# K and V loaded group by group in 32 KB runs, with scores without mask, in a decode step of attention beside an MLP

## The chip, the cores and the metric

The kernel runs on one core of a Trainium2 chip. A core has five engines that run side by side and meet through semaphores: TensorE (PE), VectorE (DVE), ScalarE (ACT), GpSimd (POOL) and SyncE (SP), and 16 DMA engines that bring data from HBM into SBUF (128 partitions). Matmuls write into PSUM (128 partitions, 8 banks of 512 fp32). The metric is the device time of one execution in microseconds.

## The reference

One token (batch 1, length 1, D = 1024) goes through an attention over the last 4096 positions of a cache and an MLP, side by side; everything is bf16 in HBM.

```python
def _A_ref(x, k_cache, v_cache, wq, wo):        # Hq 32, Hkv 4, Dh 128, W = 4096, Sk = 65536
    q = (x @ wq).reshape(B, Sq, Hq, Dh).transpose(0, 2, 1, 3)
    k = repeat(k_cache[:, :, Sk - W:, :], 8, axis=1)
    v = repeat(v_cache[:, :, Sk - W:, :], 8, axis=1)
    p = softmax(einsum("bhqd,bhkd->bhqk", q, k) * Dh ** -0.5)
    o = einsum("bhqk,bhkd->bhqd", p, v)
    return o.transpose(0, 2, 1, 3).reshape(B, Sq, Hq * Dh) @ wo
def _B_ref(x, w1, b1, w2, b2):                  # F = 3584
    y = layernorm(x)
    return gelu(y @ w1 + b1) @ w2 + b2
xn = layernorm(x)
return x + _A_ref(xn, ...) + _B_ref(xn, ...)
```

The bytes that have to come in are wq 8 MB, K 4 MB, V 4 MB, w1 7 MB, W2 7 MB, wo 8 MB (MB of 1024 KB). Eight query heads share one of the four groups of K and V.

## The kernel before

All engines' programs are written out by hand, with semaphores between them. There is no scheduler: each engine runs its instructions in the order of the text, and the order of the transfers is the order in which SP issues them.

**The queue.** SP issues, in this order: wq's first half (`WQ_CHUNKS`, 4 MB), the first pair of groups of K (`load_k(0)`, L232), wq's second half, the second pair of K, w1 in one piece, then, after a wait for the last transpose of K (L311), the two pairs of V (L313, into the tile `KV` that K has left), after a wait for q the two chunks of W2 (16 and 12 of 28 rows per partition, into wq's place), and after a wait for h the five chunks of wo (L320; 8, 12, 9, 2 and 1 of 32 rows per partition). A row here is one of the 2 KB rows that a partition holds of W2 or wo. The three short rows x, b2 and b1 are issued by ACT; b1 comes as 128 pieces of 56 bytes.

**K and V before.** `pairs` lays a pair of groups over 128 partitions: partition 2m + g holds 64 positions of group g in one run of 16 KB. So a partition of a pair belongs to one of two groups, alternately.

```python
def pairs(cache, c):
    return cache[0, 2 * c:2 * c + 2, SK - W:SK, :].rearrange("g (m i) d -> m g (i d)", m=64)
```

**Start.** Two matmuls spread x over the partitions, DVE normalises it twice (L245 to L275), and writes the columns into `XZ` (for q) and `YZ` (for h). POOL makes constants. Matmuls with `HOT` (the `edge` function) clear PSUM banks 7, 0 and 1 before sums are added there.

**q and scores.** 64 matmuls give q in bank 7 (L449). DVE turns K in 32 by 32 blocks, in four pieces of 4096 columns (`turn_k`, L285): two for the first pair, then one, then the last behind q's turn. q is turned and spread into `QBD` (L305, L307). Four matmuls write a mask into banks 3 to 6 (`OTHER`, `ALT`, L455), 32 matmuls add the scores (L465) in 2048 columns. DVE takes the maximum (L334 to L343), ACT the exponential with its sums (L346), and DVE turns P into `PT` (L350), which lies at the end of `KT`.

**h.** 56 matmuls (L487) with w1, turned by four small matmuls (L494), with b1 added by DVE (L356) and the gelu behind it, give the first columns of `GO`.

**o and the output.** 32 matmuls of P and V (L502) in 8 turns of 4; DVE scales and picks (L383, L389); four small matmuls turn the result (L513) and ACT spreads it into `GO` and `OT`. W2 and wo are multiplied in rounds of 4 rows, 8 matmuls each, summed in bank 7: four rounds of W2, the turning of o, then three more of W2 and five of wo (`TURN`, `ROUNDS`; L523). POOL waits for the chunks and feeds PE's counter `s_feed`. The last 12 rows of wo (`TAIL` = 20) are multiplied by small matmuls of 32 columns, four side by side (L541), as their chunks land; the wo rows from 20 on lie in `KT`. Then ACT and DVE copy the sum out (L400) and SP stores it (L402).

Of the kernel before, what the change touches and what calls it, by code (L numbers as in the profile page):

```python
# [9 lines left out]
D = 1024  # L10
# [13 lines left out]
WO_CHUNKS = [8, 12, 9, 2, 1]  # L24
WO_HEAD = 2
XW = 136
PAIRS = 2
FAR = -1e30
XP = 72
TAIL = 20  # L30
# [5 lines left out]
ROUNDS = 12  # L36
TURN = 4
# [15 lines left out]
def bass_parallel_sum__sliding_block_cached__mixer_channel_mlp__decode_kernel(  # L53
# [19 lines left out]
    def sems(name, n):  # L73
        return [nc.alloc_semaphore(f"{name}{i}") for i in range(n)]

    s_x, s_b1, s_b2, s_v, s_out = (nc.alloc_semaphore(n) for n in ("s_x", "s_b1", "s_b2", "s_v", "s_out"))
    s_w1 = sems("s_w1", len(W1_CHUNKS))
    s_wq = sems("s_wq", len(WQ_CHUNKS))
    s_k = sems("s_k", PAIRS)
# [7 lines left out]
        "x", "h", "hT", "q", "sc", "pv", "tot", "o2", "fin")}  # L87
# [11 lines left out]
    B64 = sb("B64", [128, 64], f32)  # L99
    HALF4 = sb("HALF4", [64, 4], f32)  # L100
    HALF = sb("HALF", [64, PAIRS], f32)
    OTHER = sb("OTHER", [2, 128], bf16)
    ALT = sb("ALT", [2, 512], bf16)
    HOT = sb("HOT", [1, 8 + 128], bf16)
    EDGE = sb("EDGE", [2, 132], bf16)
    XBRP = sb("XBRP", [2, 16 * XP], bf16)
    B1T = sb("B1T", [128, FC], bf16)
# [8 lines left out]
    QBD = sb("QBD", [128, PAIRS * 512], bf16)  # L116
    HT = sb("HT", [128, FC], f32)
    U2 = sb("U2", [128, FC], f32)
    MX2 = sb("MX2", [128, 2], f32)
    MX8 = sb("MX8", [32, 8], f32)  # L120
    MXR = sb("MXR", [32, 1], f32)
    NMB = sb("NMB", [128, 1], f32)
# [6 lines left out]
    REC = sb("REC", [64, 1], f32)  # L129
    ON = sb("ON", [32, DH], bf16)  # L130
    GO = sb("GO", [128, ROUNDS * STEP + LEAD + 96], bf16)
    OT = GO[:, ROUNDS * STEP + LEAD:]
    ONM = QBD[0:32, :].bitcast(f32)
    KV = sb("KV", [128, 16384], bf16)
    KT = sb("KT", [128, 16384], bf16)
    PT = KT[:, 16384 - 2112:16384]
# [14 lines left out]
    def wo_home(row):  # L151
        return (BIG, (FC + row) * D) if row < TAIL else (KT, (row - TAIL) * D)
# [19 lines left out]
    act.dma_start(B1T[:, :], B_b1.rearrange("(p c) -> p c", c=FC)).then_inc(s_b1, 16)  # L172

    def pool_wait():
# [4 lines left out]
    POOL.mark(pool.memset(identb[:, :], 0.0))  # L179
    pool_wait()  # L180
# [5 lines left out]
    POOL.mark(pool.memset(HOT[:, :], 0.0))  # L186
    pool_wait()
    C["hot"] = POOL.mark(pool.memset(HOT[:, 7:8], 1.0))
# [3 lines left out]
    POOL.mark(pool.memset(QBD[:, :], 0.0))  # L192
    POOL.mark(pool.memset(HALF4[:, :], 1.0))
    POOL.mark(pool.memset(OTHER[:, :], FAR))
    POOL.mark(pool.memset(ALT[:, :], 0.0))
# [12 lines left out]
    POOL.mark(pool.affine_select(  # L208
        out=OTHER[:, :].rearrange("p (x g h) -> p x g h", g=2, h=REP),
        in_=OTHER[:, :].rearrange("p (x g h) -> p x g h", g=2, h=REP),  # L210
        pattern=[[0, 8], [-1, 2], [0, REP]], compare_op=ALU.not_equal, fill=0.0, base=0, channel_multiplier=1))
    POOL.mark(pool.affine_select(
        out=ALT[:, :].rearrange("p (x g) -> p x g", g=2), in_=ALT[:, :].rearrange("p (x g) -> p x g", g=2),
        pattern=[[0, 256], [-1, 2]], compare_op=ALU.not_equal, fill=1.0, base=0, channel_multiplier=1))
    POOL.mark(pool.affine_select(
        out=HALF4[:, :], in_=HALF4[:, :], pattern=[[-16, 4]], compare_op=ALU.is_ge, fill=0.0,
        base=0, channel_multiplier=1))
    pool_wait()
    POOL.mark(pool.affine_select(
        out=HALF4[:, :], in_=HALF4[:, :], pattern=[[16, 4]], compare_op=ALU.is_ge, fill=0.0,  # L220
        base=15, channel_multiplier=-1))
    POOL.mark(pool.memset(GO[:, :], 0.0))
    pool_wait()
    POOL.mark(pool.tensor_tensor(out=HALF[:, :], in0=HALF4[:, 0:2], in1=HALF4[:, 2:4], op=ALU.add))
    C["consts"] = POOL.cnt


    def pairs(cache, c):
        return cache[0, 2 * c:2 * c + 2, SK - W:SK, :].rearrange("g (m i) d -> m g (i d)", m=64)

    def load_k(c):
        sp.dma_start(KV[:, c * 8192:(c + 1) * 8192], pairs(A_k_cache, c)).then_inc(s_k[c], 16)  # L232

    load_chunks(WA, wq_p, WQ_CHUNKS[:1], NQ, s_wq)
    load_k(0)
    load_chunks(WA, wq_p, WQ_CHUNKS[1:], NQ, s_wq[1:], WQ_CHUNKS[0])
    load_k(1)
# [5 lines left out]
    def layernorm_stats(src, n, name):  # L243
# [15 lines left out]
    layernorm_stats(PS[:, 0:1024], 0, "ln1")  # L259
    DVE.mark(dve.tensor_scalar(out=XN[:, :], in0=PS[:, 0:1024], scalar1=MV[:, 0:1], scalar2=SD[:, 0:1],  # L260
# [18 lines left out]
        out=B64[:, :].rearrange("p (k r) -> p k r", k=2),  # L279
        in_=identf[:, :].rearrange("p (q r) -> p r q", q=4).unsqueeze(1).to_broadcast([128, 2, 32, 4]),  # L280
        axis=AX.X, op=ALU.add))

    def turn_k(n):
        dve.wait_ge(s_k[n // 2], 16)
        C["kt", n] = DVE.mark(dve.transpose(KT[:, n * 4096:(n + 1) * 4096], KV[:, n * 4096:(n + 1) * 4096]))  # L285

    for n in range(3):
        turn_k(n)
# [7 lines left out]
    dve.wait_ge(POOL.sem, C["consts"])  # L296
    act.wait_ge(POOL.sem, C["consts"])
    QD = QBD[:, :].rearrange("p (c e b h) -> p c e b h", c=PAIRS, e=4, b=4)
    QS = QTB.rearrange("p (j e c) -> p e c j", j=4, e=4)
    for b in range(4):  # L300
        for c in range(PAIRS):
            to = QD[32 * b:32 * b + 32, c, :, b, 16 * c:16 * c + 16].rearrange("p e (u j) -> p e u j", j=4)
            of = QS[32 * b:32 * b + 32, :, 4 * c:4 * c + 4, :]
            if PAIRS * b + c < 5:
                C["d_QBD"] = DVE.mark(dve.tensor_copy(to, of))  # L305
            else:
                C["a_QBD"] = ACT.mark(act.activation(out=to, in_=of, func=ACTF.Copy))  # L307
    turn_k(3)

    V = KV[:, :]  # L310
    sp.wait_ge(DVE.sem, C["kt", 3])  # L311
    for c in range(PAIRS):
        sp.dma_start(V[:, c * 8192:(c + 1) * 8192], pairs(A_v_cache, c)).then_inc(s_v, 16)  # L313
# [4 lines left out]
    for j, n in enumerate(WO_CHUNKS):  # L318
        home, first = wo_home(c0)
        sp.dma_start(home[:, first:first + n * D], wo_flat[:, c0 * D:(c0 + n) * D]).then_inc(s_wo[j], 16)  # L320
        c0 += n
# [9 lines left out]
    S = PS[:, 3 * 512:7 * 512]  # L331
    for n in range(2):
        dve.wait_ge(done["sc"], 14 + 2 * n)
        C["mx"] = DVE.mark(dve.tensor_reduce(  # L334
            out=MX2[:, n:n + 1], in_=S[:, 1024 * n:1024 * n + 1024], axis=AX.X, op=ALU.max))
    dve_wait()
    for b in range(4):
        DVE.mark(dve.tensor_copy(MX8[:, 2 * b:2 * b + 2], MX2[32 * b:32 * b + 32, :]))
    dve_wait()
    DVE.mark(dve.tensor_reduce(out=MXR[:, :], in_=MX8[:, :], axis=AX.X, op=ALU.max))  # L340
    dve_wait()
    for b in range(4):
        C["nmb"] = DVE.mark(dve.tensor_scalar(  # L343
            out=NMB[32 * b:32 * b + 32, :], in0=MXR[:, :], scalar1=-SCALE, scalar2=None, op0=ALU.mult))
    act.wait_ge(DVE.sem, C["nmb"])
    C["exp"] = ACT.mark(act.activation(  # L346
        out=Pb[:, :], in_=S, func=ACTF.Exp, bias=NMB[:, 0:1], scale=SCALE, accum_out=SUMP[:, 0:1]))

    dve.wait_ge(ACT.sem, C["exp"])
    C["d_pt"] = DVE.mark(dve.transpose(PT[:, 0:2048], Pb[:, :]))  # L350
# [4 lines left out]
    dve.wait_ge(s_b1, 16)  # L355
    DVE.mark(dve.tensor_tensor(  # L356
        out=HT[:, :].rearrange("p (t c) -> p c t", c=4),
        in0=PS[:, 2 * 512 + 32:2 * 512 + 64].rearrange("p (c t) -> p c t", c=4)[:, :, 0:7],
        in1=B1T[:, :].rearrange("p (t c) -> p c t", c=4), op=ALU.add))
# [18 lines left out]
    DVE.mark(dve.reciprocal(out=REC[:, :], in_=PS[0:64, 2 * 512 + 64:2 * 512 + 65]))  # L378
    dve_wait()
    dve.wait_ge(done["pv"], 8)  # L380
    for i in range(2):
        rows = slice(32 * i, 32 * i + 32)
        DVE.mark(dve.scalar_tensor_tensor(  # L383
            out=ONM.rearrange("p (i c d) -> p i c d", i=2, c=PAIRS)[:, i],
            in0=PS[rows, 512:1024].rearrange("p (c i d) -> p i c d", c=PAIRS, i=2)[:, i], scalar=REC[rows, 0:1],
            in1=HALF[rows, :].unsqueeze(2).to_broadcast([32, PAIRS, DH]), op0=ALU.mult, op1=ALU.mult))
    dve_wait()
    with nc.allow_low_precision(reason="one of the four terms is not zero"):
        C["on"] = DVE.mark(dve.tensor_reduce(  # L389
            out=ON[:, :], in_=ONM.rearrange("p (g d) -> p d g", g=4), axis=AX.X, op=ALU.add))  # L390
    act.wait_ge(done["o2"], 1)
    o2 = PS[:, 2 * 512:2 * 512 + 32]
    ACT.mark(act.activation(out=spread(FC // ROUND, TAIL // ROUND), in_=rows_of(o2[:, 0:TAIL]), func=ACTF.Copy))
    C["OT"] = ACT.mark(act.activation(
        out=OT[:, LEAD:LEAD + 2 * (32 - TAIL):2], in_=o2[:, TAIL:32], func=ACTF.Copy))
# [11 lines left out]
    pool.sem_inc(s_feed, 1)  # L407
    pool.wait_ge(s_wq[1], 16)
    pool.sem_inc(s_feed, 1)
    pool.wait_ge(DVE.sem, C["kt", 1])  # L410
    pool.sem_inc(s_feed, 1)
    pool.wait_ge(DVE.sem, C["kt", 3])
    pool.sem_inc(s_feed, 1)
    for semaphores, chunks in ((s_w2, W2_CHUNKS), (s_wo, WO_CHUNKS[:WO_HEAD])):
        if semaphores is s_wo:
            pool.wait_ge(ACT.sem, C["OT"])
        for semaphore, n in zip(semaphores, chunks):
            pool.wait_ge(semaphore, 16)
            pool.sem_inc(s_feed, n // ROUND)  # L419
    pool.wait_ge(s_wo[WO_HEAD], 16)  # L420
    pool.sem_inc(s_feed, 1)

    pe.wait_ge(POOL.sem, C["ones"])
    pe.wait_ge(s_x, 16)
    for i in range(2):
        last = pe.matmul(bank(i), lhsT=onesb[0:1, :], rhs=XB[0:1, 8 * i:8 * i + 8, :])  # L426
# [148 lines left out]
```

## Time and profile before

| what | value |
|---|---|
| median of 3 runs | 99.21 us (99.12 to 99.42) |
| profiled execution | 99.2 us, span 97.6 us |
| PE / DVE / POOL / ACT busy | 71.6 / 37.9 / 10.2 / 8.1 us |
| bytes read | 39.86 MB, 409 GB/s over the span |
| DMA share of the queue of SP | 95.7% of 16 engines' span |

The span runs from the first to the last instruction of the program in one profiled execution; the execution's own time is 1.6 us longer. Engines overlap, so busy times don't add up to the span. In the rows, `L433` is the line of the helper `add`, through which nearly all matmuls go; they are told apart by their tiles: `BIG,XZ` is q, `KT,QBD` scores, `BIG,YZ` h, `KV,KT` the product with V, `BIG,GO` the rounds of W2 and wo, `KT,GO` the last rows of wo. `SPq` is SP issuing a transfer, and `<-` names what an instruction waited for.

### The profile page before, as it was taken

What the parts mean: (1) busy time and instruction counts of PE and PEld (TensorE: products, weight loads), DVE (VectorE), ACT (ScalarE), POOL (GpSimd) and SP (SyncE); (2) the same over time, 40 slices, a digit from 0 to 9 for tenths busy, and PEclk for the clock granted to TensorE, in tenths of its full rate; (3) what the DMA queues carried; (4) which work ended last, traced back from release to release, by engine and by line L of the source; (5) the groups of instructions that cost most, each with busy time, mean ns of one, the idle gap of its engine ahead of it and who ended that gap; (6) DMA issues with size and microseconds to landing.
All of it is one profiled execution on the core that took longest, in us unless ns stands there. A gap on an engine that the chain in (4) does not pass through costs nothing.

```text
span 97.6 us, 1259 instructions
## 1 busy us (share of the span) xinstructions
PE 71.6 (73%) x337; PEld 30.1 (31%) x349; DVE 37.9 (39%) x50; ACT 8.1 (8%) x16; POOL 10.2 (10%) x29
## 2 busy tenths in 40 slices
PE   0005000399999973879979999799989999997991
PEld 0001000033444320323334444333344444443450
DVE  0001899899930699950581800050043000000001
ACT  0500000600000023000008000200000010000001
POOL 6999600000000000000000000000000000000000
PEclk9999999999999999999999999999999999999999
DMA  7599999999999998888999999999899998999980
GB/s 215 228 431 444 410 432 437 430 430 443 417 430 464 682 400 376 376 376 376 430 437 430 437 497 443 443 430 400 373 464 423 430 480 363 453 436 416 438 329 1
DMA packets 2229, 39.88 MB, mean 409 GB/s; under 512 B 434, under 2 KB 436, under 8 KB 692
## 3 DMA queue, kind: packets, MB, share of 16 engines
q1 hardware_dynamic: 2020, 39.85, 95.7%
q10 hardware_dynamic: 208, 0.01, 0.1%
q8 instruction: 1, 0.02, 0.1%
HBM read 39.86 MB, written 0.00 MB: 409 GB/s over the span
## 4 chain that ended last, share of the span: by engine, by line
DMA 79%; PE 13%; SPq 4%; issue 1%; DVE 0%
DMA BIG<-in_B_w_dram 47%; DMA KT<-in_A_wo_dram 32%; PE PS L433 13%; SPq L320 2%; SPq L232 1%; SPq L159 1%; DVE Pb L400 0%
## 5 line engine op out<-in xcount | busy, mean ns | idle before, releaser
L433 PE MATMUL PS<-BIG,GO 128*128 x84 | 20.1, 379 | 1.4 <-POOLq L419 0.5
L285 DVE STREAM_TRANSPOSE KT<-KV 128x4096 bf16<-128x4096 bf16 x4 | 17.6, 4432 | 4.8 <-DMA KV<-in_A_k_cache_dram 4.8
L433 PE MATMUL PS<-BIG,XZ 128*128 x64 | 16.2, 418 | 0.0
L433 PEld LDWEIGHTS PS<-BIG,GO 128*128 x96 | 9.3, 98 | 11.8 <-issue 1.7
L433 PE MATMUL PS<-BIG,YZ 128*128 x56 | 12.4, 380 | 0.7 <-DMA BIG<-in_B_w_dram 0.7
L433 PE MATMUL PS<-KT,QBD 128*128 x32 | 8.0, 379 | 2.6 <-DVE QBD L305 1.8
L433 PEld LDWEIGHTS PS<-BIG,XZ 128*128 x64 | 6.7, 105 | 9.9 <-issue 4.5
L400 DVE CAST Pb<-PS 64x256 bf16<-64x256 f32 x1 | 0.4, 417 | 21.7 <-PE PS L433 21.7
L433 PE MATMUL PS<-KV,KT 128*128 x32 | 8.3, 381 | 0.6
L430 PE MATMUL PS<-XBRP,HOT 1*128 1x512 bf16 x3 | 1.7, 620 | 9.0 <-DVE XZ L275 9.0
L433 PEld LDWEIGHTS PS<-BIG,YZ 128*128 x56 | 5.4, 96 | 7.5 <-issue 1.9
L426 PE MATMUL PS<-XBRP,onesb 1*128 1x512 bf16 x2 | 1.0, 605 | 8.2 <-DMA XBRP<-in_A_x_dram 8.2
L433 PEld LDWEIGHTS PS<-KT,QBD 128*128 x32 | 3.1, 96 | 7.5 <-issue 5.4
L245 DVE BATCH_NORM_STATS2 BN<-PS 128x6 f32<-128x512 f32 x2 | 1.3, 689 | 9.3 <-PE PS L426 9.3
L433 PEld LDWEIGHTS PS<-KV,KT 128*128 x32 | 3.1, 96 | 5.4 <-issue 3.9
L334 DVE TENSOR_REDUCE MX<-PS 128x1 f32<-128x1024 f32 x2 | 2.4, 1220 | 4.4 <-PE PS L433 4.4
L383 DVE SCALAR_TENSOR_TENSOR QBD<-PS,REC,HALF 32x256 f32<-32x256 f32 x2 | 0.9, 473 | 7.0 <-PE PS L433 6.9
L430 PEld LDWEIGHTS PS<-XBRP,HOT 1*128 1x128 bf16 x3 | 0.3, 118 | 10.2 <-DVE XZ L275 9.9
L350 DVE STREAM_TRANSPOSE KT<-Pb 128x2048 bf16<-128x2048 bf16 x1 | 2.3, 2312 | 2.1 <-ACT Pb L346 2.1
L356 DVE TENSOR_TENSOR HT<-PS,B1T 128x28 f32<-128x28 f32 x1 | 0.2, 209 | 7.4 <-PE PS L494 7.4
L346 ACT ACTIVATE Pb<-PS,NMB 128x2048 bf16<-128x2048 f32 x1 | 2.0, 1967 | 13.0 <-DVE NMB L343 13.0
L426 PEld LDWEIGHTS PS<-XBRP,onesb 1*128 1x128 bf16 x2 | 0.1, 98 | 8.2 <-issue 8.2
(76 smaller groups left out, 37.6 us busy)
## 6 DMA issues: line engine op xcount, KB each, us to landing
BIG<-in_A_wq_dram SPq DMA_DIRECT2D x2, 4096.0 KB, 18.9
BIG<-in_B_w_dram SPq DMA_DIRECT2D x1, 7168.0 KB, 46.0
KV<-in_A_k_cache_dram SPq DMA_DIRECT2D x2, 2048.0 KB, 23.2
KV<-in_A_v_cache_dram SPq DMA_DIRECT2D x2, 2048.0 KB, 13.4
BIG<-in_B_w_dram SPq DMA_DIRECT2D x1, 4096.0 KB, 24.6
BIG<-in_B_w_dram SPq DMA_DIRECT2D x1, 3072.0 KB, 31.2
BIG<-in_A_wo_dram SPq DMA_DIRECT2D x1, 3072.0 KB, 25.6
KT<-in_A_wo_dram SPq DMA_DIRECT2D x1, 2304.0 KB, 30.6
```

What stands on the lines that cost most here:

```text
L159: sp.dma_start(dst[:, c0 * width:(c0 + n) * width].rearrange("p (c n) -> p c n", c=n), src[:, c0:c0 + n, :],).then_inc(semaphores[j], 16)
L232: sp.dma_start(KV[:, c * 8192:(c + 1) * 8192], pairs(A_k_cache, c)).then_inc(s_k[c], 16)
L245: DVE.mark(dve.bn_stats(out=BN[:, 12 * n + 6 * i:12 * n + 6 * i + 6], in_=src[:, 512 * i:512 * i + 512]))
L285: C["kt", n] = DVE.mark(dve.transpose(KT[:, n * 4096:(n + 1) * 4096], KV[:, n * 4096:(n + 1) * 4096]))
L320: sp.dma_start(home[:, first:first + n * D], wo_flat[:, c0 * D:(c0 + n) * D]).then_inc(s_wo[j], 16)
L334: C["mx"] = DVE.mark(dve.tensor_reduce(out=MX2[:, n:n + 1], in_=S[:, 1024 * n:1024 * n + 1024], axis=AX.X, op=ALU.max))
L346: C["exp"] = ACT.mark(act.activation(out=Pb[:, :], in_=S, func=ACTF.Exp, bias=NMB[:, 0:1], scale=SCALE, accum_out=SUMP[:, 0:1]))
L350: C["d_pt"] = DVE.mark(dve.transpose(PT[:, 0:2048], Pb[:, :]))
L383: DVE.mark(dve.scalar_tensor_tensor(out=ONM.rearrange("p (i c d) -> p i c d", i=2, c=PAIRS)[:, i], in0=PS[rows, 512:1024].rearrange("p (c ...
L426: last = pe.matmul(bank(i), lhsT=onesb[0:1, :], rhs=XB[0:1, 8 * i:8 * i + 8, :])
L430: pe.matmul(bank(n), lhsT=HOT[:, 8:136], rhs=XB[0:1, 0:8, :], start=True, stop=False, skip_group_check=True)
L433: return pe.matmul(to, lhsT=lhsT, rhs=rhs, start=False, stop=False, skip_group_check=True, **place)
```

## The change

- K and V are each loaded by four DMAs, one for each group, into 32 partitions: partition 32g + m holds 128 positions of group g in one run of 32 KB. All four loads of K stand between wq's two halves and share one semaphore, for which DVE waits once; the four transposes of K follow in a row.
- Scores take no mask. `QZ` holds q so that each block of 32 output partitions belongs to one group; there are 1024 columns of scores, in banks 4 and 5, still 32 matmuls. The maximum goes through two 32 by 32 transposes.
- P becomes block-diagonal: POOL clears 4096 columns of `PT` (now the start of `KT`) after the scores, and four transposes of 32 partitions by 1024 columns write the blocks. The product with V has 32 matmuls in 4 turns of 8.
- o is scaled, picked, reduced and turned by DVE alone (six steps), without matmuls.
- ACT clears the PSUM banks by three copies in place of matmuls with `HOT`.
- b1 comes in 32 pieces of 224 bytes and is turned and added by four matmuls with `E4` ahead of the h sums.
- wo comes in 16, 11, 4 and 1 rows, all into `BIG`; the rounds are 11 (seven of W2, four of wo) in one loop, and 16 rows are left to the small matmuls.

The order of the transfers becomes: wq's first half, K (4 loads), wq's second half, w1, V (4 loads), W2 (2), wo (4).

The diff, cut to its core:

```diff
-WO_CHUNKS = [8, 12, 9, 2, 1]
-WO_HEAD = 2
+WO_CHUNKS = [16, 11, 4, 1]
+WO_HEAD = 1
-TAIL = 20
+TAIL = 16
-ROUNDS = 12
-TURN = 4
+ROUNDS = 11
...
-    act.dma_start(B1T[:, :], B_b1.rearrange("(p c) -> p c", c=FC)).then_inc(s_b1, 16)
+    act.dma_start(B1R[:, :], B_b1.rearrange("(p c) -> p c", p=32)).then_inc(s_b1, 16)
...
+    act.wait_ge(POOL.sem, C["QZ"])
+    for first in (0, 4):
+        ACT.mark(act.activation(out=PS[:, first * 512:(first + 2) * 512].rearrange("p (b n) -> p b n", b=2),
+                                in_=QZ[:, 0:512].unsqueeze(1).to_broadcast([128, 2, 512]), func=ACTF.Copy))
+    ACT.mark(act.activation(out=bank(7), in_=QZ[:, 0:512], func=ACTF.Copy))
...
-    def load_k(c):
-        sp.dma_start(KV[:, c * 8192:(c + 1) * 8192], pairs(A_k_cache, c)).then_inc(s_k[c], 16)
+    def load_groups(cache, semaphore):
+        for g in range(HKV):
+            sp.dma_start(KV[32 * g:32 * g + 32, :], cache[0, g, SK - W:SK, :].rearrange(
+                "(m i) d -> m (i d)", m=32)).then_inc(semaphore, 16)
 
     load_chunks(WA, wq_p, WQ_CHUNKS[:1], NQ, s_wq)
-    load_k(0)
+    load_groups(A_k_cache, s_k)
     load_chunks(WA, wq_p, WQ_CHUNKS[1:], NQ, s_wq[1:], WQ_CHUNKS[0])
-    load_k(1)
     load_chunks(W1, w1_p, W1_CHUNKS, F, s_w1)
...
-    def turn_k(n):
-        dve.wait_ge(s_k[n // 2], 16)
-        C["kt", n] = DVE.mark(dve.transpose(KT[:, n * 4096:(n + 1) * 4096], KV[:, n * 4096:(n + 1) * 4096]))
+    dve.wait_ge(s_k, 64)
+    for n in range(4):
+        C["kt"] = DVE.mark(dve.transpose(KT[:, n * 4096:(n + 1) * 4096], KV[:, n * 4096:(n + 1) * 4096]))
...
-    sp.wait_ge(DVE.sem, C["kt", 3])
-    for c in range(PAIRS):
-        sp.dma_start(V[:, c * 8192:(c + 1) * 8192], pairs(A_v_cache, c)).then_inc(s_v, 16)
+    sp.wait_ge(DVE.sem, C["kt"])
+    load_groups(A_v_cache, s_v)
...
-    C["d_pt"] = DVE.mark(dve.transpose(PT[:, 0:2048], Pb[:, :]))
+    dve.wait_ge(POOL.sem, C["consts"] + 1)
+    for g in range(4):
+        C["d_pt"] = DVE.mark(dve.transpose(
+            PT[32 * g:32 * g + 32, :].rearrange("p (i y) -> p i y", y=128)[:, :, 32 * g:32 * g + 32],
+            Pb[32 * g:32 * g + 32, 0:1024].rearrange("p (i m) -> p i m", m=32)))
...
+    pool.wait_ge(done["sc"], 4)
+    POOL.mark(pool.memset(PT, 0.0))
```

## Prediction

> **What bounds the kernel now.** I read the page's head, slices and queues first, then the chain that ended last, the waits of the DMA queue, and the timeline around the end and around the clock's steps.
>
> ```profile
> span 97.6 us, 1259 instructions
> PE 71.6 (73%) x337; PEld 30.1 (31%) x349; DVE 37.9 (39%) x50; ACT 8.1 (8%) x16; POOL 10.2 (10%) x29
> GB/s 215 228 431 444 410 432 437 430 430 443 417 430 464 682 400 376 376 376 376 430 437 430 437 497 443 443 430 400 373 464 423 430 480 363 453 436 416 438 329 1
> q1 hardware_dynamic: 2020, 39.85, 95.7%
> HBM read 39.86 MB, written 0.00 MB: 409 GB/s over the span
> DMA 79%; PE 13%; SPq 4%; issue 1%; DVE 0%
> ```
>
> One queue, SP's, moves all 39.85 MB and is busy for 95.7% of the span; no compute engine comes near. The rate is flat from the third slice to the last but one.
>
> ```profile
> SPq L313 <- DVE KT L285: 39.0, 1, 39.0
> SPq L320 <- PE PS L433: 16.9, 1, 16.9
> ```
>
> SP issues each transfer long before its turn, so these waits cost nothing. V is issued at 42.94 us and w1, ahead of it, is still arriving at 49.0; wo is issued at 62.16 and W2 runs until 75.7.
>
> ```profile
> 49.68 12.45 PE L433 MATMUL PS<-BIG,YZ 128*128 x56 [0.68 <-DMA BIG<-in_B_w_dram]
> 88.56 5.13 PE L433 MATMUL PS<-BIG,GO 128*128 x21 [0.53 <-POOLq L419]
> 93.81 1.48 PE L433 MATMUL PS<-KT,GO 128*32 128x256 bf16 x44
> 95.52 0.29 PE L433 MATMUL PS<-KT,GO 128*32 128x256 bf16 x4 [0.22 <-DMA KT<-in_A_wo_dram]
> ```
>
> At the end PE is only just behind: each row waits for a wo chunk. So the time is the sum of the queue's packets plus about 2.4 us of end. The packet records of the trace give that sum. All 16 DMA engines work at once, and in each size nearly every packet takes the same time: 2 KB 84 ns, 4 KB 159, 16 KB 611, 18 KB 686, 24 KB 912, 32 KB 1213, 56 KB 2116. Every 128-row load gives each engine 8 packets. Per engine: wq, and W2's first chunk, 3 x 1213; K and V, 4 x 611; w1 2116; W2's second chunk 912; wo 611 + 912 + 686 + 159 + 84 = 2452: together 11,563, times 8 = 92.5 us. The first packet starts at 1.84, the first ones take up to 2173 ns, and the last lands at 95.18: the sum closes to 0.1 us. The span adds 2.37 us behind that, and the execution's 99.2 us is 1.6 over its span; it equals the median, 99.21.
>
> **The change, part by part.**
>
> *K and V loads.* Before, a K or V load writes all 128 partitions in 16 KB runs; after, it writes 32 partitions in 32 KB runs, four loads in a row. Each of the 16 engines gets 2 packets of 32 KB per load, 8 for K and 8 for V. If a packet keeps its 1213 ns, K and V cost 16 x 1213 = 19.4 us instead of 32 x 611 = 19.55: a gain of 0.14. But the trace has no large load into a quarter of the partitions. Its rows do not say whether 27.0 GB/s per engine is a limit of the stream or of the place it writes to, because in every big load each engine has 8 of the 128 partitions to itself. So the packet is bounded from both sides: 1213 ns if the limit is in the stream; 4 x 1213 = 4852 ns if it is in the place, and 16 streams crowd on a quarter of the places. A gain beyond 0.14 us is excluded, since no packet in the trace is faster than its size class. I take the mildest crowding that there can be, two streams on one place, 2426 ns, midway between the ends by ratio. I take crowding rather than none because times equal to the nanosecond over all 128 packets of a load, with 16 engines running, look like a fixed path that each stream owns, and the new loads take the separateness of the partitions away: all engines write group 0 together, then group 1, then 2, then 3. They keep step, because all have equal packets in the same order; the trace shows them at most 0.5 us apart where one load ends and the next begins. So loads queued behind cannot fill in. Added per engine: 16 x 1213 = 19.4 us.
>
> [...]
>
> *wo in 16, 11, 4, 1.* Per engine 1213 + 838 (686 x 22/18) + 310 (2 x 159, less a little) + 84 = 2445, against 2452: 8 x 7 ns = 0.06 us less.
>
> *The queue's sum.* 19.4 - 0.14 - 0.06 = +19.2 us; the last packet lands at 114.4 instead of 95.2.
>
> *Whether the queue ever runs dry.* K ends at 12.64 + 19.4 = 32.0. DVE now waits for all four K loads at once; behind that wait on DVE lie the four KT transposes and, behind them, the q transpose. Four at 4.43 us (L285) end at 50.1. SP's V issue waits for them, and w1 runs until 58.7, so 8 us are spare. Four K issues in place of one put about 2 us of SP work ahead of wq's second half, which is not due before 32. W2 waits behind V for q: wq's second half lands at 41.7, and 32 matmuls take 6.9 us at 215 ns, 13.7 at 427, so at most 56. wo waits for h: scores, then h's 12.45 us, end by 79, and W2 runs until 95. All covered. The cover for V is the thinnest: gone, each late microsecond costs one.
>
> *Scores, softmax, P.* The 32 score matmuls stay; 4 mask matmuls (1.03 us) and half the score columns go. Two maxima of 1.22 us become one, eight small copies and scalings (1.4) become two small transposes, a reduce and a scaling (about 0.8); the exponential over 1024 instead of 2048 columns takes 1.0 instead of 1.97. New: POOL clears 4096 columns of PT after the scores, 3.7 us by XZ's 0.99 for 1088, and behind it on POOL are only the feeds for W2, due at 87; four transposes of P of 1024 columns, 1.16 each by L350's 2312 for 2048, together 4.6 instead of 2.3. PV needs P only when V is there (78), so 15 us cover this. PV in 4 turns of 8 instead of 8 of 4 saves four loop gaps of 0.24 us; V's landing sets its start. The o chain is now six DVE steps and no matmuls, about 3 us, and its result is needed at 105.
>
> *Start.* Three ACT copies clear PSUM (1.0, 1.0 and 0.6 us by L346's rate) and the built code has one more table load (1.28). They start near 2.8 and end near 8; ACT's first square root is due at 10.85. The two edge matmuls ahead of q (1.03) go. POOL loses its 2.3 us select on ALT and some memsets. None of it touches the queue. b1 in 32 pieces makes 96 fewer packets of about 11 ns over 16 engines: under 0.1 us.
>
> *The end.* wo's first chunk now lands 9.8 us before the last packet, T. With the 0.74 us from landing to PE seen at 88.56, four rounds of 8 matmuls at 215 ns end at T - 2.2; the 11-row chunk (44 small matmuls, 1.45 us) at T - 0.75; the 4-row chunk, there at T - 0.15, at T + 0.4; the last row was there at T + 0.34 before. So +0.06 us.
>
> *PE's clock.* With DMA stretched, PE rests from 101.0 (24 matmuls after W2's last chunk) to 105.3. The rows:
>
> ```profile
> 20.00 0.15 PEld L433 LDWEIGHTS PS<-BIG,XZ 128*128 x1 [0.28 <-issue]
> 20.43 0.15 PEld L433 LDWEIGHTS PS<-BIG,XZ 128*128 x1 [0.28 <-issue]
> 39.30 0.91 PE L433 MATMUL PS<-KT,QBD 128*128 x3 [1.76 <-DVE QBD L305]
> ```
>
> After 9 us of rest matmuls run 427 ns apart until 23.84; after 1.76 us they run at 215. A rest of 4.3 us is nearer the second; I take no loss. If half speed returns, up to 4 to 5 us of the 6.9 us of rounds double, and with the slack of the end it costs up to 2.0 us, which I keep for the range. [...]
>
> **Sum.** 99.2 + 19.2 + 0.06 = 118.5 us.
>
> **Rivals.**
>
> *Streams keep their rate (not slower).* The limit is in the engine, so a packet takes 1213 ns wherever it goes. Then the queue's sum falls by 0.2, the end adds 0.06: 99.0 us. For it: 27.0 GB/s holds for all sizes and rows. Against: no row has several engines on one place. It decides if a 32 KB packet of K takes under 1250 ns. PE is then the second bound: q's second half could not start before 32.7 instead of about 28, scores end near 52, h near 64.8, PV near 73.4, W2's rounds near 85.4, while wo's first chunk is ready at 86.1; 0.7 us are spare, so with a slow clock after the rest of 6 us in q it could be 99.0 to 99.8.
>
> *A quarter.* Each engine's share of a 32-row load falls on the same few places: 4852 ns a packet, +58 us, 157 us. For it: 32 of 128 partitions is a quarter. Against: the two rows of an engine need not lie at the places of the others.
>
> *Something between or late.* A crowding that the engines partly evade, or V late: 103 to 117 or 121 to 140.
>
> **Chances.** Two on a place 0.68, full rate 0.20, quarter 0.06, between or late 0.06. What a measurement of this kernel can tell from no change is about 0.3%, 0.3 us. Full rate splits into 0.04 faster, 0.11 same, 0.05 slower; all else is slower: 0.04, 0.11, 0.85. The likeliest case's own range is 117.6 (the engines' 0.5 us of skew used once at each of K and V) to 121 (the clock falls, packets slightly over double). To leave out no more than 2 in 10 the range must reach to the full rate: 98.9 to 121.
>
> **What would show it.** Right: K's four loads landing about 19 us after wq's first half, near 32 us; slices of about 215 GB/s there and again for V between 59 and 78; slices over 400 elsewhere; V issued near 50; a chain that still ends in wo's last row. Wrong: K landed near 22 and rates over 400 throughout (full rate), or K landed near 51 (quarter); a queue idle between w1 and V would put the cost on DVE's transposes and not on the loads.

## The result and the profile after

The changed kernel takes 121.69 us (median of 6, 121.0 to 122.72) against 99.23: a ratio of 1.227, 95% interval 1.2208 to 1.2331. Slower, as forecast; the forecast of 118.5 is 3.2 us short, and the range, which goes to 121, ends 0.7 us too early. The profiled execution (122.72, the slowest of the six) has a span of 121.4.

The page's head, the granted clock and the rates in 40 slices of 3.03 us, the queue, and the chain that ended last:

```profile
span 121.4 us, 1227 instructions
PEclk9999999999755555996799999965799999965799
GB/s 173 411 455 379 314 173 173 216 227 248 173 410 453 459 491 302 605 302 605 173 173 227 238 227 173 173 345 443 421 432 397 456 443 421 443 393 438 391 165 1
q1 hardware_dynamic: 1684, 39.85, 94.9%
DMA 58%; PE 34%; issue 2%; SPq 2%; DVE 1%; ACT 1%; POOLq 0%
```

The same 39.85 MB, the same queue at 95%, but two valleys near 200 GB/s: slices 6 to 11, where K arrives, and 20 to 26, where V does. Between them the rate is what it was. SP's waits and the timeline around V's issue show that the queue did not run dry:

```profile
SPq L209 <- DVE KT L266: 46.9, 1, 46.9
```

```profile
33.63 17.42 DVE L266 STREAM_TRANSPOSE KT<-KV 128x4096 bf16<-128x4096 bf16 x4 [14.62 <-DMA KV<-in_A_k_cache_dram]
51.08 1.72 SPq L209 DMA_DIRECT2D KV<-in_A_v_cache_dram  x4
```

V is issued at 51.1 and w1, ahead of it, ends at 59.7. By the packet records, K's and V's packets of 32 KB take 2564 ns (median; wq's 1213 in the same trace), so the last packet lands at 116.85 instead of 95.18: +21.67. The end behind it takes 4.55 us instead of 2.37: +2.18. Together 23.85, the difference of the spans. The timeline of the end:

```profile
107.84 1.46 PE L403 MATMUL PS<-BIG,GO 128*128 x3 [4.20 <-POOLq L393]
108.24 0.15 PEld L403 LDWEIGHTS PS<-BIG,GO 128*128 x1 [0.15 <-issue]
108.67 0.15 PEld L403 LDWEIGHTS PS<-BIG,GO 128*128 x1 [0.27 <-issue]
109.09 0.15 PEld L403 LDWEIGHTS PS<-BIG,GO 128*128 x1 [0.28 <-issue]
117.75 1.65 PEld L403 LDWEIGHTS PS<-BIG,GO 128*32 128x32 bf16 x64 [0.42 <-issue]
119.73 0.42 DVE L376 CAST Pb<-PS 64x256 bf16<-64x256 f32 x1 [25.93 <-PE PS L403]
```

PE rests 4.2 us before wo's first round and then loads weights every 427 ns, the slow spacing of the start of the kernel before. The `PEclk` row has the same at its right end: 9, 6, 5, 7, 9. So wo's rounds end at 117.7, after the last packet, and all 64 small matmuls come behind it.

### The profile page after: what moved, and what is told of

It is laid out like the page before. It is cut to its first block, busy times and chain, and to the rows that moved or that the text cites. A ratio compares the mean times of both kernels' runs of the same rounds, so it can differ in the third digit from the quotient of the medians.

```text
span 121.4 us, 1227 instructions
## 1 busy us (share of the span) xinstructions
PE 76.0 (63%) x339; PEld 32.1 (26%) x350; DVE 40.9 (34%) x48; ACT 10.8 (9%) x19; POOL 9.3 (8%) x21
## 3 DMA queue, kind: packets, MB, share of 16 engines
q1 hardware_dynamic: 1684, 39.85, 94.9%
## 4 chain that ended last, share of the span: by engine, by line
DMA 58%; PE 34%; issue 2%; SPq 2%; DVE 1%; ACT 1%; POOLq 0%
PE PS L403 34%; DMA BIG<-in_A_wq_dram 33%; DMA BIG<-in_A_wo_dram 25%; SPq L209 2%; DVE Pb L271 1%; ACT Pb L269 0%; ACT QZ L282 0%; DVE Pb L376 0%; SPq L153 0%; POOLq L393 0%; POOLq L385 0%
## 5 line engine op out<-in xcount | busy, mean ns | idle before, releaser
L403 PE MATMUL PS<-BIG,XZ 128*128 x64 | 19.4, 478 | 25.0 <-POOLq L385 14.8
L403 PE MATMUL PS<-BIG,GO 128*128 (+1 forms) x141 | 23.8, 353 | 5.1 <-POOLq L393 4.2
L403 PEld LDWEIGHTS PS<-BIG,GO 128*128 (+1 forms) x152 | 10.9, 102 | 18.2 <-issue 11.7
L403 PE MATMUL PS<-KV,KT 128*128 x32 | 9.6, 476 | 3.4 <-DMA KV<-in_A_v_cache_dram 3.4
L403 PE MATMUL PS<-KT,QZ 128*128 x32 | 8.7, 438 | 1.2 <-ACT QZ L282 1.2
L387 POOL MEMSET KT<- 128x4096 bf16 x1 | 3.5, 3518 | 57.9 <-PE PS L403 57.9
L324 DVE STREAM_TRANSPOSE KT<-Pb 32x1024 bf16<-32x1024 bf16 x4 | 4.9, 1236 | 1.4 <-ACT Pb L318 1.3
L403 PEld LDWEIGHTS PS<-KT,QZ 128*128 x32 | 3.5, 110 | 6.3 <-issue 3.7
L306 DVE TENSOR_REDUCE MX<-PS 128x1 f32<-128x1024 f32 x1 | 1.2, 1225 | 9.4 <-PE PS L403 9.4
L318 ACT ACTIVATE Pb<-PS,NMT 128x1024 bf16<-128x1024 f32 x1 | 1.1, 1114 | 13.1 <-DVE NMT L316 13.1
## 6 DMA issues: line engine op xcount, KB each, us to landing
KV<-in_A_v_cache_dram SPq DMA_DIRECT2D x4, 1024.0 KB, 21.7
```

The source lines that it names most:

```text
L306: DVE.mark(dve.tensor_reduce(out=MX[:, 0:1], in_=S, axis=AX.X, op=ALU.max))
L318: C["exp"] = ACT.mark(act.activation(out=Pb[:, 0:1024], in_=S, func=ACTF.Exp, bias=NMT[:, 0:1], scale=SCALE, accum_out=SUMP[:, 0:1]))
L324: C["d_pt"] = DVE.mark(dve.transpose(PT[32 * g:32 * g + 32, :].rearrange("p (i y) -> p i y", y=128)[:, :, 32 * g:32 * g + 32], Pb[32 * g:3 ...
L387: POOL.mark(pool.memset(PT, 0.0))
L403: return pe.matmul(to, lhsT=lhsT, rhs=rhs, start=False, stop=False, skip_group_check=True, **place)
```

## The experiments

Theory (**place**): a load into 32 neighbouring partitions gives the 16 engines half as many places to write to, two engines share one, and packets take twice as long: an assumption made from 2564 ns against 1213. Rivals: **run** (the 32 KB run, or that all engines read one group's 1 MB), **number** (each further load costs), **rest** (the rest of the change), and for the end: the slow **clock** against the 16 rows of small matmuls.

**The loads alone.** `cut_rows` is the kernel before with each pair load cut in four:

```diff
-        sp.dma_start(KV[:, c * 8192:(c + 1) * 8192], pairs(A_k_cache, c)).then_inc(s_k[c], 16)
+        for b in range(4):
+            sp.dma_start(KV[32 * b:32 * b + 32, c * 8192:(c + 1) * 8192], pairs(A_k_cache, c)[16 * b:16 * b + 16]).then_inc(s_k[c], 16)
```

(V likewise; the waits count four loads. In the kernels below, too, the waits count the loads.)

> The kernel before with one thing changed: each of its four loads of K and V is cut by rows into four loads of 32 partitions; every byte still comes from and goes to the same place, in the same 16 KB runs. Place theory (32 partitions give 16 engines only half the places to write to): the 16 KB packets of K and V take 1282 ns instead of 611, half of the 2564 ns that 32 KB packets took in the changed kernel, so the queue grows by 32 x 0.67 = 21.5 us: 120.5 to 122.5, and 32 KB packets of wq stay at 1213. Run theory (what costs is a run of 32 KB, or one group's 1 MB read by all engines at once): 99.2 to 99.5, packets at 611. Number theory (each further load costs by itself): 12 further loads; if they cost what 16 loads cost in the changed kernel, 1 to 2 us each, 111 to 123, with packets unchanged at 611 and gaps between loads.

Measured: 120.61 us, ratio 1.2169 (1.2095 to 1.2244). 16 KB packets of K and V take 1262 to 1277 ns instead of 611, wq's stay at 1213. The slices of the page:

```profile
GB/s 176 353 519 364 260 194 231 375 353 518 298 226 198 325 463 309 559 366 309 408 220 209 209 231 198 226 369 353 518 369 455 422 408 430 446 455 409 409 270 1
```

The valleys are there with the same bytes, places and runs as in the kernel before. Run is out.

`cut_cols` makes as many loads, but over all partitions:

```diff
+        for b in range(4):
+            x = slice(2048 * b, 2048 * b + 2048)
+            sp.dma_start(KV[:, c * 8192:(c + 1) * 8192][:, x], pairs(A_k_cache, c)[:, :, x]).then_inc(s_k[c], 16)
```

> The kernel before with each load of K and V cut by columns into four loads of 128 partitions, 4 KB runs. As many loads as with the cut by rows. Place theory: 4 KB packets take 159 ns, 32 x 4 x 159 = 20.4 us instead of 19.55: 99.5 to 100.5. Run theory: the same. Number theory: as much as the cut by rows, 111 to 123.

Measured: 100.43 us, ratio 1.0132 (1.0102 to 1.0163); its 4 KB packets take 159 ns as expected, which explains 0.8 of the 1.2 us. Number is out as the main cause.

**All of the change but the narrow loads.** `all128`:

```diff
-        for g in range(HKV):
-            sp.dma_start(KV[32 * g:32 * g + 32, :], cache[0, g, SK - W:SK, :].rearrange("(m i) d -> m (i d)", m=32)).then_inc(semaphore, 16)
+        sp.dma_start(KV[:, :], cache[0, :, SK - W:SK, :].rearrange("g (m i) d -> m g (i d)", m=32)).then_inc(semaphore, 16)
```

> The changed kernel with K and V each in one load over 128 partitions, still in 32 KB runs (partition 4m + g in place of 32g + m, so groups are mixed and the values are others); all else of the change stays. Place theory: packets at 1213 ns, the queue's sum 0.2 us under the kernel before, end as there: 98.8 to 99.8. Run theory: the runs of 32 KB stay, so packets at 2564 and about 121.7. Rest theory (something in scores, softmax or the end costs): whatever is left over 99.2 is its share.

Measured: 99.02 us (98.88 to 99.93), ratio 1.000 (0.9973 to 1.0028), packets 1213. With wide loads of 32 KB runs, the new scores, P, o, b1 and wo chunks cost nothing that can be told. Rest is out.

**How many partitions.** `p64` and `p16` load 64 and 16 partitions at a time (these two, `stride4`, `v_two_queues` and `k_on_act` were run once each):

```diff
+        for j in range(2):
+            sp.dma_start(KV[64 * j:64 * j + 64, :], cache[0, 2 * j:2 * j + 2, SK - W:SK, :].rearrange("g (m i) d -> m g (i d)", m=32)).then_inc(semaphore, 16)
```

```diff
+        for g in range(2 * HKV):
+            sp.dma_start(KV[16 * g:16 * g + 16, :], cache[0, g // 2, SK - W + g % 2 * 2048:SK - W + g % 2 * 2048 + 2048, :].rearrange("(m i) d -> m (i d)", m=16)).then_inc(semaphore, 16)
```

> The changed kernel with K and V in two loads each of 64 partitions (two groups mixed, so the values are others), 32 KB runs. [...] Place theory by count of partitions (each four, or each eight, partitions a place of its own): packets at 1213, 99 to 100. Number theory: half the further loads, about 110.

> The changed kernel with K and V in eight loads each of 16 partitions, 32 KB runs, every byte to the same place as there. Place theory: half the places again, so four engines to a place and packets near 2 x 2564 = 5128 ns: 16 x 2.56 = 41 us more than the changed kernel, about 162. A fixed penalty for any load of fewer than 128 partitions: packets at 2564, about 122. Number theory: 8 further loads, by its own price of 1.4 us each about 133 to 144.

Measured: 64 partitions 121.25 us with packets of 2565, the same as 32; 16 partitions 152.49 us with packets of 4376 and 4404, 3.6 times 1213. `p16`'s slices:

```profile
GB/s 208 451 435 166 130 139 139 113 104 95 121 121 156 442 442 555 364 364 486 381 95 95 113 113 139 139 139 95 95 321 442 392 423 451 416 416 437 435 366 16
```

So the price falls in steps and not with the count: 16 cost 3.6 times 1213, 32 and 64 both 2.1, 128 one. A place for every four or eight partitions, which would have had `p64` at 1213, is out. K's 4 MB took 36 us in `p16`, 116 GB/s, and 20.65 us in the changed kernel, 203. My 162 for `p16` was 10 us too high. The engines of `p16` are up to 2.3 us out of step; that early ones then overlap with the next load of 16, if it goes to other places, is argued, not shown.

**Which partitions.** `stride4` keeps 32 rows a load and spreads them:

```diff
-            sp.dma_start(KV[32 * g:32 * g + 32, :], ...
+            sp.dma_start(KV[g:128:4, :], ...
```

> The changed kernel with each group's load of 32 partitions spread over the whole height: partition 4m + g in place of 32g + m, so groups are mixed and the values are others. Four loads of 32 rows each, 32 KB runs, as there. Place theory: the 32 partitions now reach all places, so packets come down, to 1213 if each engine's row has a place of its own at any one time (99 to 100), or stay near 2564 if the engines that run in step still meet in pairs (121 to 122). A penalty for the count of 32 rows alone: 2564, 121.7. So only a low time tells the two apart.

Measured: 98.97 us, packets 1213. Its slices:

```profile
GB/s 215 282 430 430 431 431 430 430 456 456 430 456 564 470 376 376 376 376 470 483 430 443 430 430 416 430 430 379 413 403 537 430 430 430 362 443 443 346 346 1
```

No valley, with the same four loads of 32 rows and 32 KB. It was which partitions a load holds, 1213 ns against 2564, not how many, how long its runs are or where it reads. This run tells the most. No trace names the engine that carries a row or the place that it writes to, so that two engines share one place is inferred from the times, and why engines in step don't meet in pairs at a step of 4 stays open.

**Can the halves be made to overlap?** `order` issues groups 0, 2, 1, 3 (`for g in (0, 2, 1, 3)`); `after_again` is the changed kernel beside it.

> The changed kernel with K's and V's loads issued in the order of groups 0, 2, 1, 3, so that the half of the partitions changes at each load and not once. Place theory with engines at most 1 us out of step: three changes instead of one let early engines run alone for a moment, 0 to 1 us less per set of four, 119.5 to 122.5 and most packets still near 2564. If engines drift apart freely, packets come down towards 1213 and the time to 105 to 115. A penalty by the count of rows: no change, 121.0 to 122.7.

> The changed kernel itself, on the same chip as the three kernels sent with it: 121.0 to 122.7 as measured before, packets of K and V at 2564 ns.

Measured: 120.57 us, ratio 1.2144 (1.2128 to 1.2161), against 121.34 and 1.2234 (1.2192 to 1.2276) for the changed kernel; packets 2516. Three changes of half in place of one win 0.8 us (the last packet lands at 115.94 against 116.60), and packets stay near 2564: by that the engines keep step. In the profiled execution of the changed kernel the last packets of K on the 16 engines end within 1.0 us (31.74 to 32.70).

`v_two_queues` and `k_on_act` use ACT's queue as well:

```diff
+    act.wait_ge(DVE.sem, C["kt"])
+    load_groups(A_v_cache, s_v, act, (2, 3))
...
-    load_groups(A_v_cache, s_v)
+    load_groups(A_v_cache, s_v, sp, (0, 1))
```

```diff
-    load_groups(A_k_cache, s_k)
+    load_groups(A_k_cache, s_k, act)
```

> The changed kernel with V's groups 0 and 1 issued by SP and its groups 2 and 3 by ACT, so that both halves of the partitions have loads waiting at each engine at the same time. Engines in step that take the queues in turn: all write the same half at any one time, V still takes 20.7 us, 121 to 123. If the two queues overlap within an engine, both halves are written at once: V takes about 10.5 us and the time is 111 to 113.

> The changed kernel with K's four loads issued by ACT, on a second queue, so that each engine takes K's packets and wq's in turn. Place theory with engines in step: K's packets still meet in pairs, the sum of the work stays, 120 to 123. If the two queues put the engines out of step, an engine that writes K has its place to itself while its partner writes wq: K's packets come down towards 1213 and up to 10 us are won, 111 to 120.

Measured: 121.08 us for the first, its last packet at 116.4 as without the second queue. ACT's half of V began during w1, its packets taking 2345 ns beside w1's, so the two halves of V met less than I meant, and the run says only that the sum stays. The second took 130.32 us, outside both expectations: K's packets took about 2150 ns between wq's and w1's; the last of them ended at 46.6, the loads' last completion came at 49.6, and the transposes ended at 67.1. Its slices:

```profile
GB/s 163 489 346 470 325 214 437 163 325 325 325 285 430 180 285 569 285 569 0 0 0 315 173 163 203 285 163 325 346 468 407 419 475 427 397 427 447 386 361 1
```

Three slices without a byte: w1 had ended at 59.7 and V's first packet came at 68.1. The prediction had called V's cover the thinnest; this run takes it away, and 8.3 us of dry queue put the last packet 8.7 us later. Up to there the second queue had won nothing: w1 ended at 59.7 in the changed kernel as well, so wq, K and w1 together took as long on two queues as on one.

**The end.** Three kernels take PE's rest away. `wo_split` cuts wo's first chunk (`WO_CHUNKS = [8, 8, 11, 4, 1]`, `WO_HEAD = 2`), `warm` fills the rest:

```diff
+        if first:
+            for i in range(16):
+                pe.matmul(bank(3), lhsT=identb[:, :], rhs=QZ[:, 0:512], start=True, stop=True, skip_group_check=True)
```

> The changed kernel with wo's first chunk of 16 rows cut in 8 and 8, so that PE has rounds to do from about 103.7 and does not rest 4.2 us before wo. Clock theory (PE falls to half speed in that rest and the end loses about 2.2 us): matmuls of wo's rounds 216 ns apart, end 2.4 us behind the last packet as in the kernel before, 119.2 to 120.0. Rival (the end of 4.5 us comes from the 16 rows left to the small matmuls): 121.0 to 122.0 as in the changed kernel.

> The changed kernel with 16 matmuls that nobody reads put between W2's last round and wo's first (3.45 us, into a bank that is free), so that PE does not rest there; chunks and small matmuls as in the changed kernel. Clock theory: wo's 32 round matmuls stay 216 ns apart, the end behind the last packet falls from 4.55 to 2.4 to 2.7 us, the time to 119.2 to 120.2. Rival (the longer end comes from the 16 rows of small matmuls, or the last packets themselves are late): 121.0 to 122.7.

Measured: 122.26 and 122.28 us, no better than the changed kernel (121.69 and 121.34). Yet in `warm` the round matmuls are 216 ns apart and the end behind the last packet is 2.5 us: what the clock theory wanted. But the last packet came at 118.0, 1.4 us late. The timeline of `warm`:

```profile
103.01 3.62 PE L468 MATMUL PS<-QZ,identb 128*128 128x512 bf16 x16
109.05 9.71 PE L403 MATMUL PS<-BIG,GO 128*128 x96 [2.42 <-POOLq L393]
```

The last packet of wo's first chunk ended at 106.6, but PE begins at 109.05. In between, at 106.58, the instruction queue's one packet (16 KB, 1076 ns) appears, and one DMA engine's packets of wo are up to 1.4 us late from there on. POOL waits for all 16 completions of a chunk: of this one's, 15 came by 107.04 and the last at 108.75. In the changed kernel this packet comes at 116.81, with the last data. `wo_split` has it at 114.20 and one engine late as well (last packet 117.64); there the clock fell too, at 114.7, behind a rest of 2.7 us before the 11-row chunk. That the added or moved PE work had brought the fetch into the stream is inferred; no run moves the fetch alone. So `paced` leaves PE's program alone and lets POOL feed W2's last rounds one by one:

```diff
+            if semaphore is s_w2[1]:
+                for i in range(n // ROUND):
+                    POOL.mark(pool.memset(KT[:, 8192:8192 + 2560], 0.0))
+                    pool_wait()
+                    pool.sem_inc(s_feed, 1)
```

> The changed kernel with POOL feeding W2's last three rounds one by one, with a clearing of 2560 unused columns (about 2.2 us) ahead of each, so that PE rests less than 1.5 us at a time before wo; PE's own program has the same instructions. Clock theory: wo's round matmuls 216 ns apart, the instruction fetch stays behind the last packet, which lands near 116.7 as in the changed kernel, and the end behind it is 2.4 to 2.7 us: span 119.0 to 119.5, time 120.3 to 120.8, with less spread than the changed kernel has. Rival (16 rows of small matmuls make the end): end of 3.3 to 4.6 us behind the last packet, 121.0 to 122.7.

> The changed kernel on the same chip as the paced one: 121.0 to 122.7, end 3.3 to 4.6 us behind the last packet.

Measured on one chip: paced 120.50 us (120.34 to 120.56), ratio 1.213 (1.2105 to 1.2154); the changed kernel 121.74 (121.1 to 122.7), ratio 1.2254 (1.2204 to 1.2304). The timeline of `paced`:

```profile
104.93 1.90 PE L409 MATMUL PS<-BIG,GO 128*128 x7 [0.48 <-POOLq L397]
107.61 1.41 PEld L409 LDWEIGHTS PS<-BIG,GO 128*128 x8 [1.28 <-issue]
109.42 1.41 PEld L409 LDWEIGHTS PS<-BIG,GO 128*128 x8 [0.40 <-issue]
116.55 0.92 PE L409 MATMUL PS<-BIG,GO 128*32 128x256 bf16 x20 [0.27 <-DMA BIG<-in_A_wo_dram]
```

Eight weight loads in 1.41 us, the last rows wait for DMA again, and the end is 2.5 us behind the last packet (116.67, against 116.57 in `after_pair`). The slow clock is worth 1.24 us in the median; and without it the spread falls from 1.6 us to 0.2. The granted clock of `after_pair`, `after_again` and `paced`, in this order, has a dip near its right end that is wide in the first, narrow in the second and missing in the third:

```profile
PEclk9999999999655555996799999955799999955799
PEclk9999999999955555799599999995999999995999
PEclk9999999999965555999999999955799999999999
```

No version here beats both kernels: `all128` and `stride4` reach 99.0 with groups mixed, so they show the cost of the loads and are no replacement.

## Why the prediction was right or wrong

Two steps failed: the size of the term for K and V (2.2 of the 3.2 us missed), and PE's clock, which was put at nothing (1.2).

*Queue as the bound, V's cover, scores, softmax, o, start:* right. V was issued 8.6 us before w1 ended (8 forecast), K's landing let DVE start at 33.6, and `all128` puts all the work beside the loads at no cost. That cover was real: `k_on_act`. A reading beside it is loose: 27.0 GB/s does not hold for all sizes, since the prediction's own packet times give 24.4 at 2 KB and 25.8 at 4 KB; no sum rests on it.

*K and V loads:* the runs fit the mechanism, two streams on one place, in step (2564 ns a packet for 32 neighbours, 1213 in `stride4`), though the places themselves are inferred. The factor of two was a choice, the mildest crowding between the two ends; by the rows alone, that it came near is in part luck. The term was mis-sized, and this is the larger step that failed: packets of 2564 ns, not 2426. 16 x 138 ns = 2.2 us of the 3.2 us missed. `p64` has the same 2565 and `cut_rows` 1276 for 16 KB, 2.09 times 611, so the excess grows with the bytes and is no fixed price of a packet. Why a packet takes 5% more than double (2564 against 2426) stays open.

*PE's clock:* the other step that failed. It named the rest (101.0 to 105.3; it was 103.6 to 107.8), put its price at up to 2.0 and took none, because 4.3 us lay nearer to the rest of 1.76 after which PE stayed fast. `paced` measures 1.24 in the median, and the profiled execution lost about 2. So the chain that ended last did not end in wo's last row, as forecast, but ran through PE's rounds from 107.84 on.

The clock records of the traces say why the price varies. In those of the profiled execution the clock changes between 1.0 and 0.5, and the changes lie whole multiples of 3.41 us apart (the last three at 86.44, 106.92 and 113.75 us). Eight traces have this rest of 4.2 us (three of the changed kernel, `k_on_act`, `order`, `p16`, `p64`, `v_two_queues`). The clock fell in all eight, each time at the end of a stretch of 3.41 us; in seven of them matmuls had still run for 0.1 to 1.2 us of that stretch. In six of the eight the clock stayed low for one such stretch, and 3.3 to 3.4 us lay between the last packet and the end; in the other two, both of executions above 122.5 us, it stayed low for two stretches, and it was 4.5 us. In `paced` it is 2.5. So the rest costs 0.8 or 2.0 us, which fits the spread of 1.7 us; the other executions have no trace that would show which it was.

So seven of the eight stretches that ended with the fall were not wholly idle, and the rest of 4.2 us brought it in all eight traces. By what rule the clock falls, no run here shows.

*The sum:* 118.5 + 2.2 + 1.2 = 121.9, against 121.69. In the profiled execution the last packet was 21.7 us later (19.2 forecast) and the end 2.2 longer (0.06 forecast).

*The range:* its upper end took in the clock but only "packets slightly over double"; both at once passed it. The full-rate rival had 0.20 and was wrong by almost 23 us; what spoke against it, that no row has several engines on one place, was the point.

## What to carry to other kernels

Where the time is the sum of one queue's packets, cost a load by the partitions that it writes at one time: 128, or 32 at a step of 4, ran at 27.0 GB/s per engine, 32 or 64 neighbours at 12.8, 16 neighbours at 7.5 (32 KB runs; for 32 neighbours 16 KB runs gave 12.8 too). Loads queued behind did not fill the gap: three changes of half in place of one won 0.8 us (`order`). Neither did a second queue in the two ways tried here (121.08 and 130.32 us). When the transfers stretch, look for the new rests on the other engines and price PE's slow clock with them, 1.24 us here.

## What was not expected of the hardware

- 32 rows a load ran at full rate when spread at a step of 4 partitions (1213 ns a packet) and at half when they lay together (2564).
- One instruction fetch of 16 KB took 1.08 us (0.93 in the kernel before). With the last data, at 116.81, it cost nothing that shows; in `warm` it came in the stream of wo, at 106.58, and from there on one engine was up to 1.4 us late, and the last packet with it.
- A small DVE instruction ended only with a POOL clearing that ran beside it. In the changed kernel the scaling of 32 columns takes 1.83 us and ends with POOL's memset (68.17 against 68.13), while the reduce before it takes 0.21:

```profile
64.61 3.52 POOL L387 MEMSET KT<- 128x4096 bf16 x1 [57.95 <-PE PS L403]
66.10 0.21 DVE L310 TENSOR_REDUCE MX<-MXT 128x8 f32<-128x32 f32 x1
66.34 1.83 DVE L312 TENSOR_SCALAR NM<-MX 128x32 f32<-128x32 f32 x1
68.20 0.21 DVE L316 STREAM_TRANSPOSE NMT<-NM 128x32 f32<-128x32 f32 x1
```

That these two share something is inferred from the times. It cost nothing here: P was ready at 74.7 and V at 81.
